# First loads without waits, V's scales once per batch, narrower first scores, and a new written-out order in a one-core attention and MLP kernel

## The chip, the cores and the metric

The kernel runs on one core of a Trainium2 chip. The metric is the device time of one execution in microseconds (us). A time is called changed when it differs by more than 0.2%, which is about 2 us here.

## What is computed

Three stages in a row, all inputs and outputs float32:

```python
# q, k, v: (4 batches, 8 heads, 576 positions, 64); f: (4, 8, 576)
scores = q @ k.T / sqrt(64) + cum[:, None] - cum[None, :]   # cum = cumsum(log(clip(f, 1e-4, 1)))
attn   = softmax(causal(scores)) @ v
x = attn.transpose(0, 2, 1, 3).reshape(2304, 512)
x = relu(x @ moe_w_in) ** 2 @ moe_w_out                      # 512 -> 2048 -> 512
g, val = x @ moe2_w_gate, x @ moe2_w_val                     # 512 -> 1536
out = (silu(g) * val) @ moe2_w_out                           # 1536 -> 512
```

## The kernel before

The weights reach the device as 64-bit words. A quarter of W_in (there are four, `i` 0 to 3) is loaded in two pieces of 1024 KB. Each piece is turned into float32 by two ScalarE instructions (`top_half` L362, `low_half` L365) and one on VectorE (`join` L370); TensorE takes a bound of its norm (`gram` L391), and after a scale was found the quarter is split into a high and a low float16 part (L450 on ScalarE, L454 on VectorE). W_out (`o`) and the three matrices of the last stage go the same way. Products of the MLP are three float16 matmuls each (high by high, high by low, low by high).

Attention is cut into 32 units, one for a batch and a pair of heads (`pr`), in two halves. The early half takes the first 256 positions as two tiles of 128 queries, `i` = 1 and then `i` = 0; the late half takes the rest. A unit loads K, Q and its rows of the decay sums (`bias`, L697), masks the diagonal on GpSimd (L754), takes the scores on TensorE (L770), adds the decay and finds the row maximum on VectorE (L793), takes the exponential on ScalarE (L813). In batches 0 and 1 of the early half (`WHOLE` = 2) the probabilities are scaled and transposed by TensorE against a diagonal matrix (`across`, L847), copied out of PSUM (`carry`, L854 on ScalarE for tile `i` = 1 or L856 on VectorE for tile 0), multiplied with raw V (L911), and written as a high and a low part of X (L946, L951). TensorE takes K and Q of the early half in full float32; a matmul of that type stands in the trace as two records.

The decay sums are made once: `f` is loaded (L261), clipped, its logarithm is taken on ScalarE (L281), scanned on VectorE (L265), stored to a table in device memory (`cum_d`, L283) and read back as `bias` by every unit.

V of a unit comes in two loads, `load_v` (256 KB, L561) and `load_v2` (its last 64 rows, L564), and the gap is zeroed on GpSimd (L604). From V its largest element (`v_max`, L567), the mean of it over the partitions by a matmul with ones (`v_mean`, L574) and four small VectorE instructions (`v_scale`, L578 to L583) follow, for each unit. All four units of a batch go into a bound, by which X of the batch is scaled.

X of 256 positions is one tile of the first MLP (`mlp1`): tiles 0 to 3 are the early half of each batch, 4 to 7 and 8 the late half. `mlp1(j)` has eight pairs of W_in columns: the first product L1119, relu and square on ScalarE, a float16 high part on ScalarE and its low part on GpSimd (`g_lo`, L1165), the second product L1187. The square needs the scales of all quarters of W_in and W_out (`cc1`). Until those are there, tiles 0 and 1 store their first product. The second MLP (`mlp2`) has five rounds; it forms sums of weight blocks on GpSimd (L489), splits them (L524, L527), multiplies (L1382) and takes the second product (L1498).

The order of all work on all engines is made by the program before anything is built: every step has an engine, an estimated duration, the steps that it depends on, the buffers that it takes and a priority. `Plan.order()` plays the steps through in time, and on each engine the ready step of the smallest priority number goes next. The instructions are then issued in that order (`manual_schedule`), and each engine runs its own in order. All loads go through one queue, SyncE's (SP). A dependency in `deps` means that the plan waits for the end of a step, one in `order` only for its start. `EPRI`, `VPRI`, `IPRI` and `OPRI` are the priorities of the early units, of V by batch, and of the quarters of W_in and W_out; `ILOAD` and `OLOAD` those of the weights' loads. Within W_in each piece's load also waits in the plan for the start of the previous piece's `top_half` (`came`).

Of the kernel before, what the change touches and what calls it, by code (L numbers as in the profile page):

```python
# [19 lines left out]
AFTER = {PE: 0.25, ACT: 0.2, DVE: 0.15, POOL: 0.2, SP: 0.0, None: 0.0}  # L20
DMA_ISSUE = 0.45
DMA_LATENCY = 1.8
DMA_RATE = 290e3
LAG1 = 2
TURN_COST = 2.0
# [4 lines left out]
}  # L30
SLOW = {DVE: 0.8, POOL: 0.35}
TURN_LATE = 3.0
LAG2 = 1
PACE = {"i": 1, "o": 3, "f": 1, "g": 1, "v": 1}
HELD = 0
# [20 lines left out]
class Plan:  # L56
# [19 lines left out]
    def order(self):  # L76
        now, dma_free = 0.0, 0.0
        free = {e: 0.0 for e in AFTER}
        hot = {DVE: 0.0, POOL: 0.0}
        cands = {e: [] for e in AFTER}  # L80
        rings, events, left = {}, [], len(self.steps)
# [16 lines left out]
        while left:  # L98
            moved = False
            for e in free:  # L100
# [14 lines left out]
                if e == SP:  # L115
                    free[e] = now + st.us
                    dma_free = max(free[e], dma_free) + st.nbytes / DMA_RATE
                    st.done = dma_free + DMA_LATENCY + st.late
                else:
                    us = st.us  # L120
                    if st.hot:
                        other = hot[POOL if e == DVE else DVE] - now
                        us += SLOW[e] * max(0.0, min(us, other))
                        hot[e] = now + us
                    free[e] = now + us
                    st.done = now + us + AFTER[e]
# [18 lines left out]
def act_us(n):  # L145
    return 0.28 + n * 0.00072


def dve_us(n):
    return 0.18 + n * 0.00106  # L150
# [6 lines left out]
def pool_us(n):  # L157
    return 0.1 + n * 0.0021
# [3 lines left out]
GATE0 = -2  # L162
GATE = 6
EPRI = [0, -10, 35, 35, 120, 132, 85, 58, 115, 42, 148, 324, 287, 324, 433, 420]
VPRI = [36, 78, 425, 71]
IPRI, ILOAD = [40, 67, 57, 83], [-153, -150, -66, -103]
OPRI, OLOAD = [210, 237, 255, 235], [78, 120, 160, 37]
VERBOSE = False
WHOLE = 2
COPY = (ACT, DVE)  # L170
ROUNDS = [(0, 1), (8,), (2, 3), (4, 5), (6, 7)]
# [4 lines left out]
def decay_attention_moe_kernel(ctx: ExitStack, tc, q, k, v, f, w1, w2, wg, wv, wo, outT):  # L176
# [25 lines left out]
    VTN = 4  # L202
    VRN = 5
    GN = 2
# [136 lines left out]
    def stage(nm, u, places, pri, lpri, deps=(), gates=(), where="hp"):  # L341
# [6 lines left out]
        for tag, nb, make, nk in places:  # L348
# [20 lines left out]
            def join(piece=piece):  # L369
# [5 lines left out]
                             order=[prev(tag), *gates, *paced(nm), *came[-PACE[nm]:][:1]]), tag)  # L375
            s1 = add(ACT, act_us(n), top_half, [ld], pri, use=[buf])
            s2 = add(ACT, act_us(n), low_half, [ld], pri, use=[buf])
            came.append(s1)
# [88 lines left out]
    def split7(c, idx, slot, scaled):  # L467
# [19 lines left out]
        def tt(out, x, y, op):  # L487
            def sum_of():
                nc.gpsimd.tensor_tensor(out(), x(), y(), op=op)  # L489

            return sum_of

        o0, e0, o1, e1 = (lambda: odd(p0)), (lambda: even(p0)), (lambda: odd(p1)), (lambda: even(p1))
        s1, s2, s3, s4 = (lambda: part(p0, 0)), (lambda: part(p0, 1)), (lambda: part(p1, 0)), (lambda: part(p1, 1))
        t1 = add(POOL, 0.2 + pool_us(512), tt(s1, o0, o1, ALU.add), [j0, j1], pri, use=[r0, r1])
        t2 = add(POOL, 0.2 + pool_us(512), tt(s2, s1, e0, ALU.subtract), [t1], pri, use=[r0])
        t3 = add(POOL, 0.2 + pool_us(512), tt(s3, e0, o0, ALU.subtract), [j0, j1], pri, use=[r0, r1])
        t4 = add(POOL, 0.2 + pool_us(512), tt(s4, e1, s2, ALU.subtract), [t2], pri, use=[r0, r1])

# [45 lines left out]
    VUNIT = {}  # L545

    def v_unit(b, pr, early, opened, pri):
        c = {}
# [22 lines left out]

        def v_mean():
            c["ps"] = ps_h.tile([P, 512], F32, tag="h", name="ps")
            nc.tensor.matmul(c["ps"][:, 0:1], ones, vmax[:, i : i + 1], start=True, stop=True)  # L574

        def v_scale():
            vm = small.tile([P, 4], F32, tag="vm", name="vm")
            nc.vector.tensor_scalar(vm[:, 1:2], c["ps"][:, 0:1], 1e-30, None, op0=ALU.max)  # L578
            nc.vector.tensor_scalar(
                vm[:, 2:3].bitcast(I32), vm[:, 1:2].bitcast(I32), 0x7F800000, None, op0=ALU.bitwise_and  # L580
            )
            nc.vector.tensor_scalar(sc[:, 1:2], vm[:, 2:3], 1.0 / PSCALE, None, op0=ALU.mult)
            nc.vector.reciprocal(sc[:, 0:1], vm[:, 2:3])  # L583

        def v_views():
# [11 lines left out]
        def v_lo():  # L597
# [4 lines left out]
                         order=[prev(vr.tag)]), vr.tag)  # L602
        lv2 = add(SP, DMA_ISSUE, load_v2, [lv], pri, use=[vr], nbytes=32000)
        lv3 = add(POOL, 0.27, lambda: nc.gpsimd.memset(c["vr"][64:128, TAIL, :], 0.0), [lv], pri, use=[vr])  # L604
        vin = [lv, lv2, lv3]
        if early:
            pbuf = Buf("hp", HN)
            c["max"] = a = add(DVE, 0.81, v_max, [*vin, ready0], pri, use=[vr])
            a = add(PE, 0.2, v_mean, [a], pri, take=[pbuf])
            SCALED[b, pr] = add(DVE, 0.6, v_scale, [a], pri, use=[pbuf])  # L610
        if whole:
            c["in"], c["buf"] = vin, vr
            return c
        c["hi"] = chained(add(ACT, act_us(nkb * P), v_hi, [SCALED[b, pr], *vin], pri, take=[VT], use=[vr],
                              order=[prev(VT.tag)]), VT.tag)
# [4 lines left out]
    def v_batch(b, pri):  # L620
        n0 = b * NP
        for pr in range(NP):
            VUNIT[b, pr] = v_unit(b, pr, True, None, pri)

        def bound(ps):
# [20 lines left out]
    def attn_unit(idx, b, pr, half, opened):  # L646
# [88 lines left out]
        for ti, i in enumerate(tiles):  # L735
# [9 lines left out]
            ng = heads[1][5] + 1  # L745
            cuts = [(0, max(ext, 256))] if ext <= 512 else [(0, ext // 2), (ext // 2, ext)]
            cg_buf = Buf("cg", 6)
# [13 lines left out]
            for ci, (n0, n1) in enumerate(cuts):  # L761
# [21 lines left out]
                for (h, r0, r1, _, _, g), mk, pbuf in zip(heads, masks, pbufs):  # L783
                    new = ci == 0 and (h == 0 or g == 1)

                    def soft(st=st, g=g, h=h, r0=r0, r1=r1, n0=n0, n1=n1, ti=ti, ci=ci, ext=ext, new=new):
# [13 lines left out]
                    sf = add(  # L800
                        DVE, 0.08 + dve_us(min(n1, ext) - n0), soft, [mm, mk, *softs[h][-1:]], pri - HELD,
                        use=[pbuf, bias, sbufs[g], cg_buf], order=[prev("soft")],
# [6 lines left out]
            for g in range(ng):  # L809

                def expo(st=st, g=g, ext=ext, mc=mc):
                    cg, s = st["cg"][:, g], st["s", g]
                    nc.scalar.activation(  # L813
                        s[:, :ext], s[:, :ext], AF.Exp, bias=cg[:, mc : mc + 1], scale=-1.0,
                        accum_out=cg[:, 2:3],
                    )

                done = softs[g] if ng == 2 else [*softs[0], *softs[1]]
                exps.append(add(ACT, 0.08 + act_us(ext), expo, done, pri, use=[sbufs[g], cg_buf]))

# [37 lines left out]
            if whole:  # L858
                dg = take(POOL, 0.1 + pool_us(256), diagonal, [sm], [p_buf], use=[cg_buf])
                a_buf = Buf("ps_at", AN)  # L860
                tn = take(PE, 0.1 + 2 * nb * 0.36, across, [dg], [a_buf, t_buf], use=[*sbufs, p_buf])
                tn = add(COPY[ti], act_us(256 * nb) if COPY[ti] == ACT else dve_us(256 * nb), carry, [tn], pri, use=[a_buf, t_buf])
# [44 lines left out]
            def mix(st=st, i=i, nb=nb, w=w, ti=ti):  # L907
# [7 lines left out]
                for blk in range(nb if not whole else 0):  # L915
                    K = min(P, S - blk * P)
                    for a, va in ((0, 0), (0, 1), (1, 0)):
# [14 lines left out]
            pbuf = Buf("ps_at", AN)  # L932
            mx = add(PE, 0.1 + nb * 0.4 if whole else 0.2 + nb * 6 * 0.03, mix, [tn, *vu["in"], XSTAT[xk], opened], pri,
                     take=[pbuf])
# [21 lines left out]
            if opens:  # L956
                kh_ = take(ACT, act_us(w) + 0.09, keep_hi, [mx, XSTAT[xk]], [xb], use=[pbuf], p=pri - HELD)
                XFIRST[xk] = kh_
            else:
                kh_ = add(ACT, act_us(w) + 0.09, keep_hi, [mx, XSTAT[xk]], pri - HELD, use=[pbuf, xb], order=[XFIRST[xk]])  # L960
            kl_ = add(DVE, dve_us(w), keep_lo, [kh_], pri - HELD, use=[pbuf, xb])
# [88 lines left out]
    for u, ab in enumerate([("o0", "o1"), ("o2", "o3"), ("f0", "f1"), ("f2", "v2")]):  # L1050
        ild = own_scale("i", u, halves(*ab), IPRI[u], ILOAD[u], gates=[BIAS[0]], where="acc")
    x2x2 = [("x2", 1, lambda: mlp.tile([P, 2048], I32, tag="x2", name="x2"), 2)]
# [47 lines left out]
    def mlp_pair(t, j, p, np_, names, lag, xs, xbuf, xdeps):  # L1100
# [42 lines left out]
        def a2():  # L1143
            h, al = G[k0][0], AL[:, p // 2 : p // 2 + 1]
            if j >= 2 * B - 1:
                nc.vector.scalar_tensor_tensor(h, h, A2[:, p // 2 : p // 2 + 1], h, op0=ALU.mult, op1=ALU.mult)  # L1146
            else:
                nc.scalar.activation(h, h, AF.Square, scale=al)

        own = not tag or first  # L1150
        r = add(ACT, act_us(512), a1, [hps[0][1]], -100, take=[tmp] if own else (),
                use=[hps[0][0], *(() if own else [tmp])], order=[prev(tag) if first else None])
        if first:
            chained(r, tag)
        if j >= 2 * B - 1:
            r = add(DVE, dve_us(512), a2, [r, cc1], -100, use=[tmp])
        else:
            r = add(ACT, act_us(512) + 0.09, a2, [r, cc1], -100, use=[tmp])

# [6 lines left out]

        h = add(ACT, act_us(512), g_hi, [r], -100, take=[gb], use=[tmp])
        l = add(POOL, pool_us(512), g_lo, [h], -100, use=[tmp, gb])
# [519 lines left out]
```

## Time and profile before

| | |
|---|---|
| three runs | 990.27, 991.50, 991.52 us, median 991.5 |
| the profiled execution | 990.59 us, of which the span of its instructions is 988.7 us |
| busy | TensorE 943.7 us (95%), VectorE 621.1 (63%), ScalarE 601.2 (61%), GpSimd 349.9 (35%) |
| DMA | 117.46 MB, all loads by one queue |

The span goes from the first to the last instruction. An engine can be waiting in a stretch where its share of the whole looks small, so the rows below are of stretches.

### The profile page before, as it was taken

To read this page: it belongs to the slowest core of one execution; us is meant where nothing else is said; L and a number is where in the kernel's file an instruction comes from. 1 tells how busy PE (TensorE), PEld (TensorE's weight loads), DVE (VectorE), ACT (ScalarE), POOL (GpSimd) and SP (SyncE) were. 2 spreads that over 40 slices of the span, in tenths; PEclk is the share of its full clock that TensorE was granted. 3 is DMA by queue.
4 is the path that set the end of the run, shared out by engine and by line. 5 is a ranking of instruction groups with operands and counts; after the bars stand their busy time and mean duration, and the time that the engine had idled before them with its cause. 6 is when DMAs were issued, how large, how long until landed. Compare 5 with 4: busy or idle time off the path is not lost.

```text
span 988.7 us, 22473 instructions
## 1 busy us (share of the span) xinstructions
PE 943.7 (95%) x8887; PEld 737.5 (75%) x8887; DVE 621.1 (63%) x1441; ACT 601.2 (61%) x1136; POOL 349.9 (35%) x440
## 2 busy tenths in 40 slices
PE   3899999999999999989999988999999999999998
PEld 2577787887778778867788877776987777777674
DVE  4788877637566677877899898336464354433332
ACT  3789897767777779877786866334443334323232
POOL 2323144154433534443286785123231222211120
PEclk9799999999999999999999999999999999999999
DMA  6896539446786689799952521000102001000101
GB/s 207 271 339 212 124 97 240 136 120 161 150 172 166 159 180 214 187 259 241 229 189 86 192 65 64 1 1 29 60 9 57 1 1 42 3 1 1 43 1 42
DMA packets 147945, 117.46 MB, mean 119 GB/s; under 512 B 98241, under 2 KB 136129, under 8 KB 142593
## 3 DMA queue, kind: packets, MB, share of 16 engines
q1 hardware_dynamic: 147840, 116.04, 44.0%
q8 instruction: 69, 1.13, 0.5%
q14 instruction: 36, 0.29, 0.1%
HBM read 83.44 MB, written 9.51 MB: 94 GB/s over the span
## 4 chain that ended last, share of the span: by engine, by line
PE 44%; DVE 4%; POOL 4%; issue 3%; DMA 1%; ACT 1%; POOLq 0%; DVEq 0%; ACTq 0%
PE acc L1498 14%; PE v L1382 13%; PE h L1382 10%; PE h L1119 3%; PE acc L1187 2%; POOL g L1165 2%; POOL raw L489 2%; DMA raw<-in_moe_w_val_dram 1%; DVE i L1325 1%; PE ps L923 1%; PE ps L770 1%; DVE tmp L1146 1%; POOL x L489 1%; DVE ms L1253 0%; DVE sq L1257 0%
## 5 line engine op out<-in xcount | busy, mean ns | idle before, releaser
L1187 PE MATMUL acc<-g,o 128*128 128x256 f16 x1728 | 208.6, 273 | 5.7 <-POOL g L1165 5.5
L1119 PE MATMUL h<-x,i 128*128 128x256 f16 x1728 | 209.1, 273 | 0.7 <-DVE pw L287 0.7
L1187 PEld LDWEIGHTS <-o 128*128 128x128 f16 x1728 | 163.2, 98 | 38.1 <-issue 17.7
L1119 PEld LDWEIGHTS <-i 128*128 128x128 f16 x1728 | 163.7, 98 | 31.1 <-issue 10.9
L1498 PE MATMUL acc<-o,f 128*128 128x512 f16 (+1 forms) x720 | 145.6, 358 | 0.5 <-ACT o L1471 0.5
L1498 PEld LDWEIGHTS <-f 128*128 128x128 f16 x720 | 70.0, 98 | 64.7 <-issue 0.8
L754 POOL TENSOR_SCALAR_AFFINE_SELECT bias<-bias 128x128 f32<-128x128 f32 (+1 forms) x160 | 63.9, 408 | 135.8 <-DVE cg L793 71.4
L1461 POOL TENSOR_TENSOR tmp<-tmp,o 128x256 f32<-128x256 f32 (+1 forms) x30 | 23.0, 766 | 249.2 <-ACT o L1455 249.2
L1165 POOL TENSOR_TENSOR g<-tmp,g 128x512 f16<-128x512 f32 x56 | 73.2, 1310 | 90.7 <-ACT g L1162 69.9
L813 ACT ACTIVATE s<-s,cg 128x128 f32<-128x128 f32 (+4 forms) x144 | 83.0, 578 | 30.5 <-DVE cg L793 29.5
L793 DVE CUSTOM_DVE_ANT_0 s<-ps,bias 128x512 f32<-128x512 f32 (+3 forms) x160 | 73.3, 480 | 43.6 <-PE ps L770 39.5
L876 DVE SCALAR_TENSOR_TENSOR p<-s,cg,p 128x512 f16<-128x512 f32 (+4 forms) x112 | 76.3, 693 | 20.2 <-ACT p L872 19.2
L1382 PEld LDWEIGHTS <-g 128*128 128x128 f16 x720 | 65.9, 98 | 12.9 <-issue 4.6
L872 ACT ACTIVATE p<-s,cg 128x512 f16<-128x512 f32 (+4 forms) x112 | 67.1, 615 | 12.3 <-issue 4.0
L1382 PE MATMUL v<-i,g 128*128 128x256 f16 (+1 forms) x540 | 68.8, 264 | 4.3 <-DVE tmp L1399 4.3
L1382 PEld LDWEIGHTS <-v 128*128 128x128 f16 x720 | 65.7, 98 | 6.8
L1427 ACT ACTIVATE r<-r,ms 128x768 f32<-128x768 f32 (+1 forms) x30 | 26.1, 870 | 72.3 <-DVE r L1399 72.2
L1382 PE MATMUL v<-i,v 128*128 128x256 f16 (+1 forms) x540 | 68.6, 264 | 0.0
L1399 DVE TENSOR_TENSOR r<-r,h 128x512 f32<-128x512 f32 (+1 forms) x30 | 19.0, 633 | 76.7 <-PE h L1382 72.2
L1465 POOL TENSOR_TENSOR r<-r,o 128x768 f32<-128x768 f32 (+1 forms) x30 | 45.6, 1519 | 42.5 <-ACT o L1458 41.8
L1399 DVE TENSOR_TENSOR r<-r,v 128x512 f32<-128x512 f32 (+1 forms) x60 | 38.0, 633 | 33.2 <-PE v L1382 31.1
L1382 PEld LDWEIGHTS <-eg 128*128 128x128 f16 x540 | 49.3, 98 | 10.5 <-issue 1.7
(185 smaller groups left out, 1632.1 us busy)
## 6 DMA issues: line engine op xcount, KB each, us to landing
raw<-in_moe_w_out_dram SPq DMA_DIRECT2D x11, 1024.0 KB, 7.4
bias<-cum_d SPq DMA_DIRECT2D x16, 576.0 KB, 5.2
raw<-in_moe_w_val_dram SPq DMA_DIRECT2D x9, 1024.0 KB, 7.1
raw<-in_moe_w_gate_dram SPq DMA_DIRECT2D x9, 1024.0 KB, 5.8
vr<-in_v_dram SPq DMA_DIRECT2D x32, 256.0 KB, 4.9
raw<-in_moe_w_in_dram SPq DMA_DIRECT2D x8, 1024.0 KB, 7.2
x_d<-tmp SPq DMA_DIRECT2D x18, 256.0 KB, 3.0
kr<-in_k_dram SPq DMA_DIRECT2D x16, 288.0 KB, 4.2
```

The lines of the kernel that those rows point to most:

```text
L754: nc.gpsimd.affine_select(diag, diag, pattern=[[-1, w]], compare_op=ALU.is_ge, fill=-8e9, base=0, channel_multiplier=1)
L793: nc.vector.tensor_tensor_reduce(out=s[r0:r1, n0:e1], in0=c["ps", ti, ci, h][r0:r1, : e1 - n0], in1=c["bias"][r0:r1, h, n0:e1], scale=-0.1 ...
L813: nc.scalar.activation(s[:, :ext], s[:, :ext], AF.Exp, bias=cg[:, mc : mc + 1], scale=-1.0, accum_out=cg[:, 2:3],)
L872: nc.scalar.activation(pv[:, 0, :ext], s[:, :ext], AF.Copy, scale=cg[:, 3:4])
L876: nc.vector.scalar_tensor_tensor(pv[:, 1, :ext], s[:, :ext], cg[:, 3:4], pv[:, 0, :ext], op0=ALU.mult, op1=ALU.subtract,)
L1119: nc.tensor.matmul(HP[key][:, u, :], w[:, wi, kk, c * P : (c + 1) * P], x[:, xi, kk, :], start=(kk == 0 and (wi, xi) == (0, 0)), stop=(kk ...
L1165: nc.gpsimd.tensor_tensor(G[k0][1][:, 1], G[k0][0], G[k0][1][:, 0], op=ALU.subtract)
L1187: nc.tensor.matmul(acc[:, d - part[0], :], w[:, wi, c, d * P : (d + 1) * P], G[k0][1][:, gi, u, :], start=(m == 0 and d == part[0] and (wi ...
L1382: nc.tensor.matmul(R[reg][:, which, :w], t[:, wh, w1_ : w1_ + P], x[:, xh, xi, kk], start=fresh and which == 0 and kk == 0 and (wh, xh) == ...
L1399: nc.vector.tensor_tensor(out(), x(), y(), op=ALU.add)
L1465: nc.gpsimd.tensor_tensor(g, g, R["g"][:, 0, 1:4], op=ALU.subtract)
L1498: nc.tensor.matmul(acc_of(d), wd[:, cc, d * P : (d + 1) * P], R["g"][:, gi, 2 * m : 2 * m + 2].rearrange("p a t -> p (a t)"), start=mm == ...
```

## The change

The second load of V and the zeroing beside it no longer wait, in the plan, for the first load; the first two quarters of W_in no longer wait for the first `bias` load, and their load priorities (-15, -17) now stand ahead of `f`, K and Q of unit 0 (-10). `v_mean` and `v_scale` go over four units at once, after the fourth `v_max`; the ring of V buffers goes from 5 to 4. The scores of tile 0 of the early half take 128 columns instead of 256. The copy out of PSUM of tile 0 goes from VectorE to ScalarE (`COPY`). The plan now knows that the ninth load waits for the first of the last eight to land (`QUEUE`), and many estimated durations and all priorities are new, so the order differs nearly everywhere. `SQUARE` = 7 names the limit that stood as `2 * B - 1`.

```diff
+QUEUE = 8
-LAG1 = 2
+LAG1 = 3
-SLOW = {DVE: 0.8, POOL: 0.35}
+SLOW = {DVE: 0.95, POOL: 0.45}
...
                     free[e] = now + st.us
+                    if len(landed) >= QUEUE:
+                        free[e] = max(free[e], landed[-QUEUE] + 0.1)
...
-GATE = 6
-EPRI = [0, -10, 35, 35, 120, 132, 85, 58, 115, 42, 148, 324, 287, 324, 433, 420]
-VPRI = [36, 78, 425, 71]
-IPRI, ILOAD = [40, 67, 57, 83], [-153, -150, -66, -103]
-OPRI, OLOAD = [210, 237, 255, 235], [78, 120, 160, 37]
+GATE = 5
+EPRI = [-10, 30, 23, 50, 38, 100, 110, 16, 120, 12, 143, 334, 297, 334, 440, 437]
+VPRI = [5, 90, 550, 178]
+IPRI, ILOAD = [60, 65, 75, 41], [-15, -17, 10, 40]
+OPRI, OLOAD = [128, 113, 177, 290], [115, 132, 180, 126]
+SQUARE = 7
+FREE = 2
-COPY = (ACT, DVE)
+COPY = (ACT, ACT)
...
-    VRN = 5
+    VRN = 4
...
+    def v_scales(b, pr, largest, pri):
+        if b not in VSTAT:
+            c, n0 = {}, b * NP
+            pbuf = Buf("hp", HN)
+            sc = vsc[:, n0 : n0 + NP]
+
+            def v_mean():
+                c["ps"] = ps_h.tile([P, 512], F32, tag="h", name="ps")
+                nc.tensor.matmul(c["ps"][:, 0:NP], ones, vmax[:, n0 : n0 + NP], start=True, stop=True)
+
+            def v_scale():
+                vm = small.tile([P, 2, NP], F32, tag="vm", name="vm")
+                nc.vector.tensor_scalar(vm[:, 0], c["ps"][:, 0:NP], 1e-30, None, op0=ALU.max)
+                nc.vector.tensor_scalar(vm[:, 1].bitcast(I32), vm[:, 0].bitcast(I32), 0x7F800000, None, op0=ALU.bitwise_and)
+                nc.vector.tensor_scalar(sc[:, :, 1], vm[:, 1], 1.0 / PSCALE, None, op0=ALU.mult)
+                nc.vector.reciprocal(sc[:, :, 0], vm[:, 1])
+
+            a = add(PE, 0.2, v_mean, [], pri, take=[pbuf])
+            VSTAT[b] = [a, add(DVE, 0.6, v_scale, [a], pri, use=[pbuf])]
...
-        lv2 = add(SP, DMA_ISSUE, load_v2, [lv], pri, use=[vr], nbytes=32000)
-        lv3 = add(POOL, 0.27, lambda: nc.gpsimd.memset(c["vr"][64:128, TAIL, :], 0.0), [lv], pri, use=[vr])
+        lv2 = add(SP, DMA_ISSUE, load_v2, [], pri, use=[vr], nbytes=32000, order=[lv])
+        lv3 = add(POOL, 0.27, lambda: nc.gpsimd.memset(c["vr"][64:128, TAIL, :], 0.0), [], pri, use=[vr], order=[lv])
...
-            cuts = [(0, max(ext, 256))] if ext <= 512 else [(0, ext // 2), (ext // 2, ext)]
+            cuts = [(0, ext if early else max(ext, 256))] if ext <= 512 else [(0, ext // 2), (ext // 2, ext)]
...
-        ild = own_scale("i", u, halves(*ab), IPRI[u], ILOAD[u], gates=[BIAS[0]], where="acc")
+        ild = own_scale("i", u, halves(*ab), IPRI[u], ILOAD[u], gates=[BIAS[0]] if u >= FREE else [], where="acc")
```

## Rows read from the trace of the kernel before

**Rows 1.** Stretches of the span: us, each engine's busy us (instructions), granted clock, DMA share, GB/s

```profile
0.00:10.00 10.00, 1.22 (x4) 0.64 (x5) 2.24 (x3) 3.25 (x3) 1.66 (x13) 1.00 0.74 202
10.00:20.00 10.00, 3.73 (x11) 1.93 (x11) 6.10 (x29) 1.40 (x5) 1.12 (x4) 1.00 0.48 171
...
50.00:60.00 10.00, 8.07 (x68) 5.71 (x67) 7.57 (x25) 6.64 (x11) 1.03 (x4) 1.00 0.98 392
...
57.00:400.00 343.00, 340.37 (x3600) 270.14 (x3598) 240.64 (x728) 278.29 (x589) 138.29 (x223) 1.00 0.69 174
...
550.00:600.00 50.00, 45.25 (x410) 39.63 (x408) 47.63 (x48) 33.73 (x42) 41.58 (x26) 1.00 0.31 111
...
750.00:800.00 50.00, 50.00 (x389) 37.82 (x387) 20.74 (x30) 15.95 (x25) 9.95 (x8) 1.00 0.01 1
```

**Rows 2.** What TensorE waited for, whole span: us, times, longest

```profile
PE ps L574 <- DVE vmax L567: 12.0, 6, 7.2
PE acc L1187 <- POOL g L1165: 5.5, 6, 1.6
```

**Rows 3.** Timeline of the head: start, duration, instruction, idle time before it and releaser

```profile
0.81 0.40 SPq L261 DMA_DIRECT2D xm<-in_f_dram  x1
...
2.65 0.45 DVE L279 TENSOR_SCALAR xm<-xm 32x576 f32<-32x576 f32 x1 [2.65 <-DMA xm<-in_f_dram]
...
3.84 1.28 ACT L813 ACT_TABLE_LOAD   x1
...
7.80 0.51 SPq L283 DMA_DIRECT2D cum_d<-xm  x1
...
11.62 1.55 DVE L567 TENSOR_REDUCE vmax<-vr 128x1 bf16<-128x640 f32 x2 [5.87 <-DMA vr<-in_v_dram]
11.97 0.37 SPq L697 DMA_DIRECT2D bias<-cum_d  x1
12.38 0.47 SPq L355 DMA_DIRECT2D raw<-in_moe_w_in_dram  x1
...
17.27 0.54 POOL L754 TENSOR_SCALAR_AFFINE_SELECT bias<-bias 128x128 f32<-128x128 f32 x2 [14.88 <-DMA bias<-cum_d]
...
18.06 0.51 ACT L813 ACTIVATE s<-s,cg 128x256 f32<-128x256 f32 x1 [12.94 <-DVE cg L793]
```

**Rows 4.** The same, where the first MLP begins

```profile
53.88 0.83 PE L1119 MATMUL h<-x,i 128*128 128x256 f16 x6
...
55.76 0.35 DVE L951 SCALAR_TENSOR_TENSOR x<-ps,xs,x 128x128 f16<-128x128 f32 x1 [1.82 <-ACT x L946]
```

**Rows 5.** ScalarE by group, 0 to 64 us: busy us, mean ns, idle before

```profile
L362 ACT ACTIVATE raw<-raw 128x1024 f32<-128x1024 f32 x8 | 9.1, 1138 | 9.1 <-DMA raw<-in_moe_w_in_dram 9.1
L365 ACT ACTIVATE raw<-raw 128x1024 int32<-128x1024 uint32 x8 | 9.1, 1136 | 0.0
```

**Rows 6.** Loads issued from 20.1 to 20.3 us: KB each, us to landing

```profile
raw<-in_moe_w_in_dram SPq DMA_DIRECT2D x1, 1024.0 KB, 5.3
qr<-in_q_dram SPq DMA_DIRECT2D x1, 128.0 KB, 5.2
```

**Rows 7.** The load issued at 19.3 us, ahead of those

```profile
kr<-in_k_dram SPq DMA_DIRECT2D x1, 128.0 KB, 2.1
```

**Rows 8.** All instructions on the tile `vm`: ns min/median/max

```profile
L579 DVE TENSOR_SCALAR vm<-vm x16: 153/154/155, 13.3 to 175.5; 128x1 int32<-128x1 int32 x16
```

**Rows 9.** TensorE's timeline, float32 matmuls of 128 columns

```profile
26.10 1.16 PE L847 MATMUL ps<-p,s 128*128 128x128 f32 x8
...
30.30 0.71 PE L847 MATMUL ps<-p,s 128*128 128x128 f32 x4
```

**Rows 10.** The copy L856, all of them

```profile
L856 DVE COPY PT<-ps x8: 403/414/425, 25.6 to 98.9; 128x256 f32<-128x256 f32 x8
```

**Rows 11.** Stretches again, one stall in the middle

```profile
420.00:430.00 10.00, 6.81 (x73) 4.84 (x70) 8.57 (x19) 7.73 (x16) 4.82 (x7) 1.00 1.14 218
430.00:440.00 10.00, 9.49 (x105) 7.19 (x106) 9.40 (x35) 6.70 (x15) 3.72 (x7) 0.83 1.12 272
```

## What the change does to the time

> **What bounds the kernel now.** I read the stretches of the span first, then what TensorE waited for, then the timeline of the head. TensorE is busy 943.7 of 988.7 us, so 45 us of its idle time are what any change of order can win, and the stretches say where they lie [rows 1]. Adding up the first 60 us by tens (six rows, of which the first two and the last stand there), TensorE was busy 38.1, idle 21.9. From 57 to 400 us it was idle 2.6 us in all, from 550 to 600 4.8 us, and in the second MLP (750 to 800 stands for it) not at all. So a gain at the head is kept as long as TensorE stays full behind it, up to the narrow place before 600 us, where VectorE is busy 47.6 and GpSimd 41.6 of 50 us.
>
> The wait that is longest in sum, 12.0 us before `v_mean` [rows 2], is not what holds the head. The chain that holds it is in the timeline [rows 3]: `f` is issued at 0.81 us and has landed at 2.65; its sums are stored from 7.80 on, the first bias load goes out at 11.97, the first mask runs at 17.27 and ScalarE's first exponential at 18.06, after 12.94 us of idling. Until then ScalarE and VectorE have next to nothing to do, and the DMA engines are at 0.48 from 10 to 20 us [rows 1], because the first W_in piece goes out only at 12.38, behind that first bias.
>
> From 17.3 us on attention of batch 0 and the W_in pieces share ScalarE and VectorE. The first MLP starts at 53.88 and goes on only after the last part of X is written, at 55.76 + 0.35 = 56.1 us [rows 4]. In these first 64 us the W_in pieces took ScalarE 9.1 + 9.1 us, and ScalarE stood 9.1 us more until their data landed [rows 5]. Being in order, it kept attention's instructions waiting behind them.
>
> **W_in ahead of everything.** By the new priorities the SP queue issues the first W_in piece first (-15), then `f`, K and Q of unit 0 (-10), V with each second load right behind its first (5), and the second piece as soon as the first one's `top_half` starts. The second quarter follows in the same way; quarters 2 and 3 keep the gate. So four pieces come in before about 24 us (an estimate: four transfers of 5.3 us [rows 6], with 1.4 MB of V, K and Q between them), and their conversion falls into ScalarE's idle time. That takes four pieces of 1.138 + 1.136 = 2.27 us, 9.1 us, out of ScalarE's stretch from 18 to 56 us, and with it half or more of the 9.1 us of waits. Not all of that shows: behind a wait that goes, the next one stands (the bias of the next unit, its mask, the join on VectorE). I take the instructions whole and about 2 us of the waits: 11 us less.
>
> Against it stands the decay chain. A load behind a W_in piece lands with it: Q, issued 0.5 us after one, took 5.2 us, the piece itself 5.3 [rows 6], while K just ahead took 2.1 [rows 7]. So `f` lands 5.2 - 2.1 = 3.1 us later, and ScalarE now runs the conversion before the logarithm, which has a table of its own: one more load of 1.28 us [rows 3] may come into the chain. The store of the sums then queues behind V and the second piece, and the first bias behind the third; in the trace before the 4.2 us from store (7.80) to bias issue (11.97) had no piece in them. Lowest 3 us later in all (only `f` waits, the rest is hidden by the store's place in the queue); highest 3.1 + 1.3 + 3.1 = 7.5. I take 4, near the low end, since the store found a queue full of V's loads before as well.
>
> The Trainium skill, page "ScalarE: Activation LUTs", section "What ACT_TABLE_LOAD costs", gives a switch of table sets 2.66 us, 1.28 for the load and 1.38 for a drain. The trace shows the 1.28 and can't show a drain, since the engine idles behind that load; by the page the chain would be 1.4 us later still, and the time 982.
>
> Sum of this part: -11 + 4 = -7 us at the start of the first MLP, 49 us instead of 56. Bounds: -9.1 - 6.1 (four of the six waits, at their mean) + 3 = -12; and if half of the 9.1 us is only shifted, +7.5 - 4.6 = +3.
>
> **V's second loads and scales.** V's data landed at 11.6 us [rows 3], 5.7 us before the first mask: loads that come earlier find the decay chain still ahead of them, so I cost them at nothing. If that cover were gone, the 7.2 us of the longest `v_mean` wait [rows 2] would count. One `v_scale` for four units takes away 12 of 16 sets of four instructions; with about 0.154 us each [rows 8] that is 48 x 0.154 = 7.4 us of VectorE up to 175 us, of which 2 or so lie in the head and are in the 11 us above. The price: the scale of a unit now waits for four V loads, and with four buffers instead of five the next batch's V begins after the first unit's product with V. Before 18 us nobody needs it; later units of batches 2 and 3 have V's priority to themselves. Nothing, with 2 us either way.
>
> **128 columns.** A float32 matmul record of 128 columns costs (1.16 - 0.71) / 4 = 0.112 us [rows 9]. A tile 0 has four records, the two heads in different rows of the array; if these run side by side, half the columns save 2 x 0.112 = 0.22 us, if not 0.45. Of 16 tiles, 4 lie in the head; the other 12 come when TensorE is full and count: 12 x 0.22 = 2.7 us. Lowest nothing (the weights' load sets the pace), highest 5.4. I take 2.7, since the heads stand in separate rows. The copy of tile 0 (0.41 us, eight times, [rows 10]) goes from VectorE to ScalarE: 3.3 us off the one and on the other, while TensorE is the full engine; four of them lie in the head, where ScalarE gets back 1.6 of the 11 us that it lost. That is within the bounds above.
>
> **The order behind the head.** Two places could move. From 420 to 440 us TensorE idled 3.19 + 0.51 = 3.7 us, and in the second half of it the granted clock was 0.83, which is 1.7 us of 10 [rows 11]: 5.4 us. And it waits 5.5 us in six pieces for GpSimd's low part of `g` [rows 2], which a larger `LAG1` can only ease as far as the two `g` buffers allow. Gone, both together give 11 us; a second such stall costs 5.4. The profile doesn't say which; I take nothing.
>
> **Sum.** 990.6 (the profiled execution, 0.9 below the median of 991.5 and within the three runs) - 7 - 2.7 = 980.9, so 981 us.
>
> **Rivals.** (a) The order also removes the stall at 420 us and part of the `g` waits: 981 - 5.4 - 2.7 (half of 5.5) = 973. For it: loads of late weights have an earlier pace (`GATE` 5). Against: the DMA engines are full there already (1.14).
>
> (b) The head is won and given back before 600 us: VectorE and GpSimd set the pace there, and a TensorE that comes earlier only waits longer, or a new stall of the size of that at 420 us opens. 981 + 7 = 988. For it: 47.6 of 50 us of VectorE [rows 1]. Against: that work is started by loads and attention, which move forward with TensorE.
>
> (c) Slower: `f` behind the W_in piece. If the chain from bias to X, and not ScalarE's load, sets the 56 us, the conversion that moved out was free, and the chain's delay counts whole: 990.6 + 6 - 2.7 = 994. It decides from the point where the first mask runs later by more than attention of batch 0 gets shorter, that is 11 us at most, or about 28 us. For it: GpSimd's mask waits for the bias at 17.27, and every later unit follows in order. Against: the 9.1 us that ScalarE waited for pieces.
>
> (d) The new loads come no earlier, because the queue is held by loads that have not landed: only the columns count, 990.6 - 2.7 = 988.
>
> **Chances.** Forecast 0.51 (its own range 976 to 986), (a) 0.16, (b) 0.16, (c) 0.14, (d) 0.03. Within 0.2% (988.6 to 992.6, what a measurement can't tell from no change) fall a third of (b) and (d) and a fifth of (c): 0.09. Slower: the rest of (c), 0.11. Faster: 0.80. Low end: half of (a) left out, 971. High end: (c) half left out, 994.
>
> **What would show it.** Right: a first W_in conversion before 8 us; a first mask later than 17.3 by 3 to 7 us; ScalarE's wait for W_in pieces well below 9.1 us; the first product of the MLP near 47 to 50 us; L770's early records of 128 columns with 0.2 us less for a tile; from there to 400 us TensorE as full as before. Wrong: a first MLP product at 55 us or later, a first mask behind 26 us, or an idle stretch of more than 5 us after 100 us that the profile before doesn't have.

## The result, and the profile after

The changed kernel takes 981.1 us (median of 4 runs, 980.8 to 981.6), the kernel before 990.9 beside it (4 runs): a ratio of 0.990, 95% interval 0.988 to 0.992. The profiled execution took 981.6 us, its span is 979.8. The predicted time was 981.0. The traces show that most of it came from another place than the prediction said.

First the head, answering to [rows 3] and [rows 4]: the timeline of the changed kernel (start, duration, instruction, idle time before it and releaser; L362 loads W_in, L369 and L372 are its conversions).

```profile
0.80 0.41 SPq L362 DMA_DIRECT2D raw<-in_moe_w_in_dram  x1
...
1.27 0.41 SPq L268 DMA_DIRECT2D xm<-in_f_dram  x1
...
6.72 1.12 ACT L369 ACTIVATE raw<-raw 128x1024 f32<-128x1024 f32 x1 [4.64 <-DMA raw<-in_moe_w_in_dram]
...
7.04 0.45 DVE L286 TENSOR_SCALAR xm<-xm 32x576 f32<-32x576 f32 x1 [7.04 <-DMA xm<-in_f_dram]
...
7.86 1.28 ACT L288 ACT_TABLE_LOAD   x1
...
9.15 0.68 ACT L288 ACTIVATE xm<-xm 32x576 f32<-32x576 f32 x1
...
11.73 0.33 SPq L290 DMA_DIRECT2D cum_d<-xm  x1
...
15.55 0.89 SPq L719 DMA_DIRECT2D bias<-cum_d  x2
...
19.47 0.54 POOL L776 TENSOR_SCALAR_AFFINE_SELECT bias<-bias 128x128 f32<-128x128 f32 x2 [17.23 <-DMA bias<-cum_d]
...
59.06 0.33 DVE L973 SCALAR_TENSOR_TENSOR x<-ps,xs,x 128x128 f16<-128x128 f32 x1
...
59.92 2.14 PE L1141 MATMUL h<-x,i 128*128 128x256 f16 x18
```

The reader is to see that the first conversion runs at 6.72 as forecast and the first mask 2.2 us later than before, but that the first product of the MLP comes at 59.9 us, not at 49: 6 us later than the 53.88 of [rows 4]. TensorE doesn't stand still for longer in front of it: up to that product it is busy 33.9 us in the kernel before and 39.6 in the changed one, so idle 20.0 and 20.4 us. The new order has put more of TensorE's other work ahead of it. ScalarE's own account of its first 64 us, answering to [rows 5]: the W_in conversions are as long as before, and the wait for their data is 12.4 us instead of 9.1.

```profile
L369 ACT ACTIVATE raw<-raw 128x1024 f32<-128x1024 f32 x9 | 10.3, 1147 | 12.4 <-DMA raw<-in_moe_w_in_dram 12.4
```

Of the 12.4 us, 7.3 lie before 17 us, where ScalarE had next to nothing else to do. From 17 to 68 us its row for these waits is:

```profile
ACT raw L369 <- DMA raw<-in_moe_w_in_dram: 5.1, 4, 2.5
```

So in the stretch that the prediction wanted relieved the wait fell from 9.1 to 5.1 us. But ScalarE does not have less to do there: from 18 to 56 us it is busy 27.8 us before and 32.3 in the changed kernel. It converts six pieces there instead of seven, and the new order has put four more exponentials (20 instead of 16) and two more splits (4 instead of 2) into it, beside the copies of tile 0.

Where the time came from is seen in stretches of both spans (columns as in [rows 1]). The kernel before:

```profile
0.00:100.00 100.00, 78.10 (x571) 57.92 (x572) 72.48 (x243) 72.26 (x140) 26.32 (x72) 0.95 0.78 257
100.00:400.00 300.00, 297.66 (x3235) 236.09 (x3234) 203.27 (x616) 238.02 (x513) 125.73 (x195) 1.00 0.68 161
400.00:500.00 100.00, 95.69 (x1104) 75.56 (x1103) 81.34 (x209) 76.92 (x151) 38.17 (x57) 0.98 0.97 231
500.00:550.00 50.00, 47.40 (x439) 41.54 (x435) 46.84 (x52) 38.87 (x47) 33.16 (x19) 1.00 0.35 122
...
600.00:650.00 50.00, 45.96 (x361) 35.87 (x359) 24.92 (x42) 21.54 (x36) 12.75 (x10) 0.97 0.08 27
```

The changed kernel, with the two rows that answer to [rows 11] behind them:

```profile
0.00:100.00 100.00, 78.16 (x573) 59.46 (x574) 69.62 (x219) 79.02 (x153) 27.20 (x74) 0.93 0.76 248
100.00:400.00 300.00, 297.39 (x3234) 237.90 (x3231) 199.04 (x587) 240.08 (x511) 127.04 (x196) 0.99 0.73 169
400.00:500.00 100.00, 96.91 (x1093) 76.05 (x1092) 80.31 (x206) 75.78 (x151) 38.11 (x54) 0.97 0.92 221
500.00:550.00 50.00, 49.64 (x466) 43.81 (x464) 47.76 (x52) 39.65 (x48) 33.51 (x21) 1.00 0.42 149
550.00:600.00 50.00, 44.91 (x407) 39.28 (x404) 49.66 (x55) 35.80 (x47) 41.00 (x26) 1.00 0.27 86
600.00:650.00 50.00, 49.99 (x389) 37.78 (x387) 26.66 (x36) 19.54 (x33) 10.92 (x9) 1.00 0.06 20
...
420.00:430.00 10.00, 7.50 (x87) 5.55 (x82) 8.20 (x26) 6.82 (x18) 3.81 (x7) 0.94 0.82 164
430.00:440.00 10.00, 9.68 (x88) 6.88 (x86) 7.96 (x24) 6.04 (x13) 2.27 (x7) 0.72 1.12 299
```

In its first 100 us TensorE is busy 78.10 us before and 78.16 after: the head gave nothing that can be seen. Single executions with the same order in these 100 us differ by up to 1.2 us (78.66 in `e3_before_turn` below, 76.97 in `e12_after_v3_earlier`), so a gain of 7 would show. It idles 4.0 us less from 600 to 650 us, 2.2 less from 500 to 550 and 1.2 less from 400 to 500; over the whole span it idles 38.0 us instead of 45.0 and is busy 941.8 instead of 943.7, which is the 8.9 us of the span. The stall at 420 us is still there. What TensorE waited for says which work let it go. Before, beside [rows 2], there was this row, a wait at 604.9 us where the second MLP begins:

```profile
PE v L1382 <- DVE tmp L1399: 4.3, 2, 4.0
```

This wait of 4.0 us costs more than itself. Behind it the granted clock is 0.50 from 609 to 612 us, and TensorE takes 4.16 us for 24 matmuls; just before, 24 like them took 2.6.

The same view after; L1209 is the old L1187, L1187 the old `g_lo`, L1404 the old L1382, L564 `v_mean`, L398 the bound of W_in (`gram`, the old L391):

```profile
PE ps L792 <- DMA qr<-in_q_dram: 7.8, 1, 7.8
PE ps L398 <- DVE raw L377: 6.7, 4, 4.6
PE ps L564 <- DVE vmax L601: 4.2, 3, 2.0
...
PE v L1404 <- DVE r L1421: 1.9, 2, 1.6
...
PE acc L1209 <- POOL g L1187: 0.6, 1, 0.6
```

The waits for `g` went from 5.5 to 0.6 us, the turn to the second MLP from 4.3 to 1.9, and `v_mean` still waits, now for all four V loads of a batch. Its waits fell from 12.0 to 4.2 us, but in the head others stand in their place: TensorE waits 7.8 us for the first Q instead of 4.0, and the bound of W_in waits 6.7 us for its pieces instead of 2.2.

### The profile page after: what moved, and what is told of

The parts are those of the page before. It is cut to its first block, busy times and chain, and to the rows that moved or that the text cites. A ratio compares the mean times of both kernels' runs of the same rounds, so it can differ in the third digit from the quotient of the medians.

```text
span 979.8 us, 22430 instructions
## 1 busy us (share of the span) xinstructions
PE 941.8 (96%) x8875; PEld 739.6 (75%) x8875; DVE 615.5 (63%) x1385; ACT 606.7 (62%) x1145; POOL 348.1 (36%) x440
## 5 line engine op out<-in xcount | busy, mean ns | idle before, releaser
L1209 PE MATMUL acc<-g,o 128*128 128x256 f16 x1728 | 209.1, 274 | 0.6 <-POOL g L1187 0.6
L1209 PEld LDWEIGHTS <-o 128*128 128x128 f16 x1728 | 163.7, 98 | 32.7 <-issue 11.8
L1187 POOL TENSOR_TENSOR g<-tmp,g 128x512 f16<-128x512 f32 x56 | 75.2, 1343 | 95.9 <-ACT g L1184 95.8
L835 ACT ACTIVATE s<-s,cg 128x256 f32<-128x256 f32 (+4 forms) x144 | 83.4, 582 | 15.1 <-DVE cg L815 14.7
L898 DVE SCALAR_TENSOR_TENSOR p<-s,cg,p 128x512 f16<-128x512 f32 (+4 forms) x112 | 74.2, 679 | 23.0 <-ACT p L894 22.3
L1404 PEld LDWEIGHTS <-g 128*128 128x128 f16 x720 | 65.4, 98 | 10.7 <-issue 2.7
L1404 PEld LDWEIGHTS <-v 128*128 128x128 f16 x720 | 65.4, 98 | 6.5
L1404 PE MATMUL v<-i,g 128*128 128x256 f16 (+1 forms) x540 | 67.9, 262 | 1.8 <-DVE r L1421 1.6
L1404 PE MATMUL v<-i,v 128*128 128x256 f16 (+1 forms) x540 | 67.9, 262 | 0.0
L1404 PEld LDWEIGHTS <-eg 128*128 128x128 f16 x540 | 49.3, 98 | 10.7 <-issue 1.8
```

The source lines that it names most:

```text
L835: nc.scalar.activation(s[:, :ext], s[:, :ext], AF.Exp, bias=cg[:, mc : mc + 1], scale=-1.0, accum_out=cg[:, 2:3],)
L898: nc.vector.scalar_tensor_tensor(pv[:, 1, :ext], s[:, :ext], cg[:, 3:4], pv[:, 0, :ext], op0=ALU.mult, op1=ALU.subtract,)
L1187: nc.gpsimd.tensor_tensor(G[k0][1][:, 1], G[k0][0], G[k0][1][:, 0], op=ALU.subtract)
L1209: nc.tensor.matmul(acc[:, d - part[0], :], w[:, wi, c, d * P : (d + 1) * P], G[k0][1][:, gi, u, :], start=(m == 0 and d == part[0] and (wi ...
L1404: nc.tensor.matmul(R[reg][:, which, :w], t[:, wh, w1_ : w1_ + P], x[:, xh, xi, kk], start=fresh and which == 0 and kk == 0 and (wh, xh) == ...
```

## The experiments

Every time is a median, beside runs of the kernel before on the same chip; ratios are to those, with a 95% interval, and can differ a little from the quotient of the medians. Where the expectations speak of theories A and B, B is the prediction and A what the two traces suggest.

**One part alone: the columns, both ways, and the turn.** `e1_after_wide` issues 256 columns again in the changed order; `e2_before_narrow` issues 128 in the order of before; `e3_before_turn` moves four steps at 595 us in the order of before: the last block sum behind the first sum that the second MLP's finish needs (`gd1`, L1461), and three X parts of round 2 (L1321) ahead of a block's split (L524) that waits for GpSimd. The first two lines below are of `e2`; `e1` has `kmax`, 256 here, in place of `ext`.

```diff
-  c["ps", ti, ci, h][:M, : n1 - n0], ..., K[rows, n0:n1]
+  c["ps", ti, ci, h][:M, : (ext if early else n1 - n0)], ..., K[rows, n0 : (ext if early else n1)]
...
     order = plan.order()
+    for a, before in [(2220, 2990), (3144, 2227), (3152, 2227), (3154, 2227)]:
+        move(a, before)
```

> The kernel after with its order as it is, and only the issued score matmuls of tile 0 back at 256 columns. The prediction's price of the narrower scores was 2.7 us (0.22 us for each of 12 tiles that lie where TensorE is full), so it expects 981 + 2.7 = 983.8. If the score's weights set the pace, or the work behind gives the time back, it stays within 0.5 of 981. Two heads that don't run side by side would give 986.

> The kernel before with its order as it is, and only the score matmuls of tile 0 of the early half at 128 columns. By the prediction 991 - 2.7 = 988.3. Rival: the turn to the second MLP near 600 us, where VectorE and GpSimd set the pace, gives it back: 990 to 991.

> The kernel before; in its order only the turn to the second MLP is changed: GpSimd's difference for the first pair goes ahead of its last block sum, and ScalarE's three first X parts of the second round go ahead of the split that waits for that sum. If the trace's 4.0 us wait of TensorE near 605 us comes from this order, and that is where a good part of the 9.8 us was won, 987 to 988. If the prediction was right that the head gave 7 us and the order behind it nothing, within 1 us of 991.

Measured: 983.2 us for wide columns in the changed kernel, ratio 0.9917 (0.9897 to 0.9937), 2.1 us above the changed kernel, though the two intervals overlap; its profiled execution, 987.6, lies far above that median, so its trace isn't read. 989.2 for narrow columns in the old order, ratio 0.9967 (0.9953 to 0.998), 2.9 us. 987.6 for the turn, ratio 0.9956 (0.9941 to 0.9971), 4.5 us. So the columns are worth 2 to 3 us; by itself only the old order shows it clear of noise. TensorE's groups of early scores in the narrow kernel (busy us, mean ns):

```profile
L770 PE MATMUL ps<-kr,qr 64*128 64x256 f32 x64 | 15.7, 493 | 5.3 <-DMA qr<-in_q_dram 4.2 <-DVE cg L793 1.1
...
L770 PE MATMUL ps<-kr,qr 64*128 64x128 f32 x64 | 10.1, 366 | 1.2 <-DVE cg L793 1.2
```

That is 25.8 us where 128 wide ones took 29.5 before: 3.7 us for 16 tiles, 0.23 for one. And the turn, with no load moved at all, is the largest single gain found; in its trace the wait before L1382 is 2.5 us instead of 4.3, and the granted clock from 600 to 620 us is 1.00 instead of 0.91. That is 1.8 us less of waiting and about 1.5 less of slow matmuls, 3.3 of the 4.5.

**The decay chain first.** `e4_after_f_first`: in the changed order `f`, its store and both biases go ahead of the W_in pieces. As the moved steps stand, the sums are stored before the scan has made them and the logarithm is taken before the clip; the other work is the same.

```diff
     order = plan.order()
+    for a, before in [(0, 152), (3, 153), (4, 9), (5, 16), (30, 171), (61, 171)]:
+        move(a, before)
```

> The kernel after; in its order only the decay chain is moved ahead: f's load before the first W_in piece, its logarithm before the first conversion, the scan before the first maximum of V, the store of the sums behind V's second unit, the first two bias loads ahead of the third W_in piece. The first mask should run at about 15 us instead of 19.5. If the head is set by that chain and TensorE stays full behind it, 977 to 978. If ScalarE's conversions or the loads set the head, or the gain is given back at the turn near 600 us, 980 to 981.

Measured: 981.9 us, ratio 0.9895 (0.9878 to 0.9911), no different from the changed kernel. The first mask runs at 16.03 instead of 19.47, but ScalarE could make no use of it:

```profile
9.96 0.68 ACT L288 ACTIVATE xm<-xm 32x576 f32<-32x576 f32 x1 [7.88 <-DMA cum_d<-xm]
...
19.15 1.12 ACT L369 ACTIVATE raw<-raw 128x1024 f32<-128x1024 f32 x1 [3.67 <-DMA raw<-in_moe_w_in_dram]
...
22.60 0.51 ACT L835 ACTIVATE s<-s,cg 128x256 f32<-128x256 f32 x1
```

The logarithm waits for the store that now stands before it, the conversions come behind it, and the third of them waits for its data in front of the first exponential, which runs at 22.60 us instead of 21.60. So this run has the mask early and not the exponentials, and the price of `f` behind the W_in piece stays open.

**Both, and a third edit.** `e5_before_both` is the old order with narrow columns and the turn; `e6_before_three` has besides seven block sums (L489) moved behind the next `g_lo` on GpSimd, with the two splits that need them.

```diff
+    for step in [(2127, 2763, 1), (2128, 2775, 1), (2159, 2799, 1), (2160, 2811, 1), (2179, 2852, 1),
+                 (2180, 2864, 1), (2187, 2180, 1), (2200, 2912, 1), (2207, 2200, 1)]:
+        move(*step)        # behind the step named
```

> The order of before with two edits at once: 128 columns for the early tile 0, and the turn to the second MLP as moved by hand in the earlier run. Theory A (what the two traces showed: columns 3.3, turn 4.4, each in a place where TensorE is the full engine, so they add): ratio 0.9967 + 0.9956 - 1 = 0.992, about 983.5 us. Theory B (the prediction: a gain of 7 us at the head, columns 2.7, the order behind the head nothing): 988 us. If the two gains overlap: 987 us.

> The same with a third edit: between 510 and 590 us GpSimd makes the low part of g ahead of seven of the block sums that stood before it. No load and nothing of the first 400 us is moved. Theory A: the waits for g (5.5 us in six pieces) go down by 2 to 3 us, so 981 us, the whole gain of the changed kernel without any of its first loads. Theory B: still 988 us, since the head is as before. If the sums are only late elsewhere: 983.5, as the run with two edits.

Measured: 984.8 us for two, ratio 0.9945 (0.9927 to 0.9964), so 6.6 us by the medians and 5.5 by the ratio: most of the two gains adds up, and it is over half of the whole gain of the change. With three 991.8, ratio 1.0007 (0.9995 to 1.0019): the third edit lost 7 us. My reading of the `g` waits was too short. What ScalarE waited for from 500 to 600 us:

```profile
ACT v L524 <- POOL raw L489: 3.5, 2, 3.0
ACT g L524 <- POOL raw L489: 3.3, 1, 3.3
```

The splits on ScalarE now wait for the late sums, and behind them stand its relus and `g` parts; TensorE is busy 6.21 of the 10 us from 560 on, and still waits 6.1 us for `g`. Moved like this, the sums cost more than the earlier `g_lo` gave.

**Planned anew with one thing changed.** `e7_first_loads_alone` is the kernel before with the first two quarters freed and put ahead of `f`; `e8_after_gated` is the changed kernel with `FREE` = 0. In both the planner makes a new order.

```diff
-IPRI, ILOAD = [40, 67, 57, 83], [-153, -150, -66, -103]
+IPRI, ILOAD = [40, 67, 57, 83], [-15, -17, -66, -103]
-        ... gates=[BIAS[0]], where="acc")
+        ... gates=[BIAS[0]] if u >= 2 else [], where="acc")
...
-FREE = 2
+FREE = 0
```

> The kernel before, with only the first two quarters of W_in freed of the wait for the first bias and put ahead of f in the queue (priorities -15 and -17), and the order made anew from that. Theory B (prediction): first MLP 7 us earlier, 984 us. Theory A (the hole in the loads only moves to 20 to 30 us, attention of batch 0 still ends at its old time): the first MLP product not before 52 us and 991 us, with 3 us either way for an order that differs elsewhere.

> The changed kernel with the first two quarters of W_in waiting for the first bias again, and the order made anew from that. Theory B (prediction): the 7 us of the head are lost, 988 us. Theory A: the same as the changed kernel, 981 us, with 3 us either way for an order that differs elsewhere; the first MLP product no later than 61 us.

Measured: 1008.7 us, ratio 1.0175 (1.0153 to 1.0197), and 1002.9, ratio 1.0127 (1.0108 to 1.0147), 22 us above the changed kernel. Both theories fell; my "3 us either way" for a new order was far too small. In the first the mask runs at 21.17 us, the MLP starts at 68.1 and TensorE is busy 69.3 of the first 100 us. The second has a head like the others (first MLP product at 57.1, busy 77.1 of 100 us) and loses most of its time in two places far behind W_in's first loads:

```profile
130.00:140.00 10.00, 3.24 (x26) 2.31 (x24) 7.83 (x31) 8.31 (x18) 2.12 (x4) 0.82 0.17 42
600.00:610.00 10.00, 0.00 (x0) 0.00 (x0) 9.12 (x6) 4.26 (x5) 10.00 (x6) 0.71 0.15 52
```

So the time of a new planning can't be put down to the edit that set it off, and the next runs keep the order and shift steps by hand.

**W_in's pieces shifted within an order.** `e9_after_w_in_later` puts the first four pieces of the changed kernel behind the biases; `e10_before_w_in_earlier` puts those of the old one 9 to 10 us earlier.

```diff
     order = plan.order()
+    # due: each step's planned start plus the shift of its piece, but never before what it needs
+    order.sort(key=lambda st: due[st.idx])
```

> The changed kernel in its own order, not planned anew: only the loads of the first two quarters of W_in go behind the first two bias loads, with their conversions, bounds and splits 8 to 15 us later; quarter 2 goes 4 to 6 us later and quarter 3 2 to 4; all else stays in its place. Theory B (prediction: W_in ahead of everything gives 7 us at the head): 988 us. Theory A (attention of batch 0, not W_in, sets the head, so the early pieces give nothing): 981 to 982 us, the first mask before 18 us, ScalarE converting its first piece at 20 us or later, and the first MLP product between 58 and 62 us all the same. A new planning gave 1003 us for a like edit; if the late pieces themselves were the cause of that, about 1000 us here too.

> The kernel before in its own order, not planned anew: only the four first W_in pieces are loaded, converted, bounded and split 9 to 10 us earlier, behind f, K and Q of the first two units and ahead of V, and those of quarters 2 and 3 6 us earlier. Theory B (prediction: 11 us of ScalarE leave its stretch from 18 to 56 us): first MLP product at 45 to 49 us, 984 us. Theory A (the head goes as fast as attention of batch 0 goes): first MLP product at 52 to 56 us, 990 to 992 us.

Measured: 988.7 us for later pieces, ratio 0.9978 (0.9969 to 0.9987), 7.6 above the changed kernel, which is theory B's number, but not its mechanism; 1001.6 for earlier pieces in the old order, ratio 1.0108 (1.0094 to 1.0122), which is nobody's. Either way a piece out of its order costs. With later pieces TensorE is busy 70.2 of the first 100 us and the first MLP product comes at 67.6. ScalarE's waits from 17 to 68 us and TensorE's from 0 to 70 us:

```profile
ACT raw L369 <- DMA raw<-in_moe_w_in_dram: 19.2, 3, 15.2
...
PE ps L792 <- DVE cg L815: 13.8, 3, 6.3
```

ScalarE stands before conversions whose data come late, with exponentials behind them. The mask is at 14.68 us and VectorE has the first maxima by 15.4, but the first exponential runs at 21.54, no earlier than in the changed kernel (21.60), since the first conversion stands ahead of it and waits until 19.13. So the run prices late pieces with their conversions in that place; late pieces with the conversions behind the first exponentials were not run. In the old order with earlier pieces the harm is on the queue:

```profile
11.56 0.51 SPq L283 DMA_DIRECT2D cum_d<-xm  x1
...
17.64 0.89 SPq L697 DMA_DIRECT2D bias<-cum_d  x2
...
21.89 1.53 POOL L754 TENSOR_SCALAR_AFFINE_SELECT bias<-bias 128x128 f32<-128x128 f32 x2 [19.50 <-DMA bias<-cum_d]
```

V's five first loads, behind the first piece, take 5.88 us to go out instead of 2.63. The second piece goes out at 10.35 and the store of the sums behind it and V's second loads, 3.8 us later than in [rows 3]; the mask is 4.6 later, the first MLP product 9.8 (63.7). That is the prediction's rival (c), a delay of the chain that counts whole, here through the store and not through `f`, and in an order not made for it.

**The conversions taken away.** `e11_before_no_conversion`: the kernel before, all else in place.

```diff
-            s1 = add(ACT, act_us(n), top_half, [ld], pri, use=[buf])
+            s1 = add(ACT, act_us(n), (lambda: None) if nm == "i" and u < 2 else top_half, [ld], pri, use=[buf])
```

> The kernel before in its own order, without the eight ScalarE conversions of the first two quarters of W_in (they are left out: the pieces are loaded with the same size from Q's array, and VectorE joins their words with another bit operation of the same length). This is the price of those conversions by itself, with f, the bias and every other load where they were. Theory B (the prediction's term: 9.1 us of instructions and 2 us of waits come out of ScalarE's stretch from 18 to 56 us and count whole): first MLP product at 43 to 45 us, 980 us. Theory A (attention of batch 0 sets the pace of the head, ScalarE has slack): first MLP product at 51 to 54 us, 988 to 991 us. Half and half: 48 us and 985 us.

Measured: 990.3 us, ratio 1.0004 (0.9989 to 1.0019). This settles the disputed cost for the old order. ScalarE was busy 28.4 us instead of 35.0 in the first 60, and the head hardly moved:

```profile
53.27 0.83 PE L1125 MATMUL h<-x,i 128*128 128x256 f16 x6
...
53.69 1.11 ACT L366 ACTIVATE raw<-raw 128x1024 f32<-128x1024 f32 x1 [2.23 <-DMA raw<-in_moe_w_in_dram]
...
54.70 0.35 ACT L952 ACTIVATE x<-ps,xs 128x128 f16<-128x128 f32 x1
...
55.09 0.35 DVE L957 SCALAR_TENSOR_TENSOR x<-ps,xs,x 128x128 f16<-128x128 f32 x1 [1.76 <-ACT x L952]
```

Nine us of ScalarE's instructions gave 0.6 us at the first product, 53.27 for 53.88, and `e3_before_turn`, whose head is that of the kernel before, has 53.39. The rows show why at this place: the last part of X stands behind a conversion of a later quarter, which waits for its data, as it did before. And over the stretch other waits took over; ScalarE's from 17 to 56 us:

```profile
ACT s L819 <- DVE cg L799: 17.3, 6, 11.9
ACT x L952 <- PE ps L917: 5.2, 4, 2.1
ACT raw L366 <- DMA raw<-in_moe_w_in_dram: 3.2, 2, 2.2
```

In the kernel before these three are 12.9, 1.1 and 9.1 us. With the conversions went 5.9 us of waits for their data, and the waits for VectorE and TensorE grew by 8.5.

**V of batch 3 earlier.** `e12_after_v3_earlier`: in the changed order three units' V loads go ahead of the transposes of `p` at 149 us.

```diff
+    for step in [(838, 775), (839, 775), (844, 775), (845, 775), (850, 775), (851, 775),
+                 (840, 838, 1), (846, 844, 1), (852, 850, 1)]:
+        move(*step)
```

> The changed kernel in its own order, except that the V loads of units 1 to 3 of batch 3 (with the zeroing beside them) go into the SP queue ahead of the transposes at 149 us instead of behind them. The wait of TensorE for the largest elements before the one v_mean of the batch (3.2 us from 64 to 200 us, 2.0 of it at 161 us) is the price of one scale for four units with four V buffers, which the prediction put at nothing. If it is real, 979 us (977.5 if the idle places behind it go too); if the transposes that now come later hold the late units, 981 us or more; by the prediction, 981 us.

Measured: 980.6 us (978.7 to 982.4), ratio 0.9892 (0.9874 to 0.9909), which can't be told from the changed kernel. The waits of TensorE from 64 to 200 us:

```profile
PE ps L945 <- DMA PT<-p: 1.3, 2, 0.7
PE ps L564 <- DVE vmax L601: 1.0, 1, 1.0
```

The wait at `v_mean` went from 3.2 to 1.0 us and 1.3 came back at the transposes that now start later.

## Why the number was right and the main step wrong

**W_in ahead of everything, -7: wrong.** The step that failed is "I take the instructions whole and about 2 us of the waits: 11 us less". The 9.1 us of conversions were costed as if ScalarE were the bound from 18 to 56 us, and in the order of before their price is 0 (ratio 1.0004). ScalarE had slack there, between waits for VectorE, TensorE and data. Nor did the new order leave the stretch emptier: ScalarE is busy 32.3 us in it instead of 27.8. What held in part is the wait for the pieces, 5.1 us there instead of 9.1, but it bought nothing. The +4 for the decay chain was about right as a delay (`f` landed 5.7 us after its issue instead of 1.8, the mask came 2.2 later, less than the 3 to 7 forecast, and the first exponential 3.5, at 21.60 for 18.06); what it costs in the changed order stays open. By the prediction's own sign, "a first MLP product at 55 us or later", the step was wrong. That sign alone would not prove it, since the new order puts other work first; the idle times before that product, 20.0 and 20.4 us, do.

Whether the new order needs the early pieces is not shown: shifted late within it they cost 7.6 us, but with a conversion in front of the first exponentials. The old order reached the same 78 us of TensorE work in 100 us with late pieces. So loads and order were changed together, and the pair is worth nothing at the head that these traces can show.

**V's second loads and scales, nothing within 2: right in size.** `v_mean` waits 3.2 us past 64 us where it waited 1.4 before, and with most of that gone the time doesn't change by what can be measured. The copy of tile 0 on ScalarE was not run by itself; in the changed trace no matmul waits for the copies (L876), and weight loads wait 1.3 us for them.

**128 columns, -2.7: right.** 2.1 us in the new order (not clear of noise by itself), 2.9 in the old, 0.23 for a tile against 0.22.

**The order behind the head, nothing: wrong.** It is where most of the gain lies. The stall at 420 us, which I named, stayed: TensorE idles 2.8 us there and the clock is at 0.72 in the second half. The `g` waits, which I named too, went (5.5 to 0.6). The turn to the second MLP at 605 us, with 4.0 us the longest single wait behind the head, I did not cost at all: it stands in no row of the prediction, and moved by hand in the old order it alone gives 4.5, the slow matmuls behind it included.

**The sum.** Columns 2 to 3, the turn 3 to 4.5, together 5.5 to 6.6 measured; the remaining 3 to 4 us lie at 500 to 550 us (TensorE 47.25 busy with two edits, 49.64 in the changed kernel) and at 600 to 650 (47.35 and 49.99), less what the changed kernel loses earlier. These were not reproduced by an edit of their own; the one that was tried lost 7, so what made them is open. That the forecast of 981 came out is luck: a gain of 7 that wasn't there stood in for one of about the same size that was: a part of rival (a) without its head.

**The page.** The Trainium skill, page "ScalarE: Activation LUTs", section "What ACT_TABLE_LOAD costs", gives a switch of tables 2.66 us. Now that the engine doesn't idle behind the load, the trace can tell: a conversion ends at 7.84, the load takes 1.28 and the logarithm starts at 9.15, 1.31 us in all. No drain of 1.38 us shows there; the measurement decides.

## What to carry to other kernels

Before an engine's instructions are costed whole, ask what that engine waits for: one that stands 9 us for data and 12.9 for a mask has slack, and taking its work away buys nothing. Where a change renews a written-out order, read every wait over 2 us of the old trace as a term, the far ones too, since any of them may go; a cost worked out for one part doesn't reach the new order. And to test one part of such a change, shift steps within the order that is there, and look in the trace for what a shifted step now stands in front of: in two of the runs above a conversion that waited for its data held the first exponentials back, and the run no longer priced the part it was made for. A new planning put 17 us on the kernel before and 22 on the changed one, and how much of that is the edit's can't be told.

## What the runs showed of the hardware

In these traces a small load right behind a big one on the same queue landed with it: the 72 KB of `f`, issued 0.47 us behind a 1024 KB piece that took 5.9 us, were there after 5.7 us, and after 1.8 where no piece went ahead. A switch of ScalarE's tables between two instructions took 1.31 us from the end of one to the start of the next. After TensorE had stood for 4.0 us at 604.9 us in the kernel before, its granted clock was 0.50, the lower of its two levels (1.2 of 2.4 GHz), from 609 to 612 us; in `e3_before_turn`, where the longest wait there is 2.3 us, it was 1.00 from 600 to 620.
